# Attention and two MLP layers on one core: values of a batch pooled earlier, PSUM banks 3 and 3, y three chunks behind h

## Chip, cores and metric

One core of a Trainium2 chip runs the whole program. The metric is device time in microseconds (us) of one execution. PE is TensorE (PEld its weight loads), DVE VectorE, ACT ScalarE, POOL GpSimd, SP SyncE.

## What is computed

The reference in short: pooled attention, a dense layer pair, and a layer pair of eight experts with one expert per token.

```python
k_p = k.reshape(8, 8, 72, 8, 64).mean(axis=3)        # keys and values pooled by 8
v_p = v.reshape(8, 8, 72, 8, 64).mean(axis=3)
attn = softmax(q @ k_p^T / 8)                        # 8 batches, 8 heads, 576 queries
x = (attn @ v_p) as [4608, 512]                      # a token's 8 heads side by side
h = x @ w_in                                         # 512 -> 2048
y = maximum(0.01 * h, h) @ w_out                     # 2048 -> 512
expert = argmax(y @ w_gate); gate = softmax(y @ w_gate)[expert]
out = gate * (maximum(y @ w1[expert], 0) @ w2[expert])   # 512 -> 1024 -> 512
```

## The kernel before

The 4608 tokens form 18 blocks of 256, and the 2048 hidden units 16 chunks of 128. One pass of the main loop (L1221) is a step: block b and chunk f. Blocks 0 and 1 take the first 32 steps together; from block 2 on step s is block s // 16, chunk s % 16. All fp32 products are made of pairs of fp32r halves, high and low.

In a step PE makes h of its chunk (`g1`, L495, 12 matmuls of 256 columns) into a PSUM bank. ACT writes 0.01 h into a tile `g`, DVE writes the maximum back into the bank (L509), ACT rounds it to the high half in a `ghl` tile (`g_hi`, L512), and DVE subtracts to get the low half (`g_lo`, L517). PE later makes the chunk's y step (`g2`, L521, 6 matmuls of 512 columns, L529) from `ghl` into banks y0 and y1. The list `pend` holds chunks whose y step is still to come; two are left over after a step, one at the last step of a block and the first of the next. `y_evac` (L536) copies a finished block's y out on ACT in step 0 of the next block.

PSUM has eight banks: two for y, and from step 38 on four for h (h0, h1, and y2 and y3, which the first two blocks' y needed) and two (a0, a1) for all else. `pt` (L124) hands the banks of a kind out in turn, by a counter modulo their number. A new user of a bank waits until the last user's readers are done.

Between h and the y steps of a step, `run_slot` issues what a table has put there (`at`, L1023; `plan`, L1026). Its entries for the attention of token tile t of 128: transposes of q (`att_a`, L361) in chunk 0 or 7, scores (`att_b`), exponential, the quotient `pn` (`att_n`, L401), its transposes (`att_c`, L412 and L418, whose results DVE takes from PSUM to `at_t`), and in chunk 15 the product with the values for the next block (`att_av`, L439). Keys and values of a batch come in seven loads: four of keys, two of values, and the last 64 rows of values. `kv_load` (L190) issues a load on SP into one of two `kv` tiles, `kv_pool` (L290) adds on DVE, three instructions each (L297), and `kv_use` (L308) writes `kT` (by a transpose, L313), `vm` (L325) and `vr`. For the last rows POOL multiplies by a mask (L300), then ACT and DVE write `vr` (`v_rest`, L332). A batch's seven uses stand four of keys first and then three of values, two steps apart:

```python
use += [use[3] + 2, use[3] + 4, use[3] + 6]
```

For batches 2, 3, 6 and 7 the last of these is step 62, 94, 206 and 238, one step ahead of the product that reads it; for batches 4 and 5 it is 135 and 167, eight steps ahead of the product.

The gate's 16 logits of a block are made on DVE (`logit`, L546), about one per step, while the next block is computed; `route_a`, `route_b` and `route_c` then make ranks and scatter the tokens into a list in DRAM. The weights of the experts are split into halves meanwhile: `ps_split` (L824) on ACT and POOL, 128 times. For the first 16 blocks a count (`early_1`) and a list (`early_2`) are made within the last block, at its chunks 7 and 12, and the rows of the first two pairs of tiles are gathered on POOL's DMA queue. After the loop come the last block's routing, 14 pairs of tiles of experts (`p_g1`, `p_h`, `p_g2`) and single tiles (`steps`).

## Time and profile before

| | us |
|---|---|
| three timed runs | 1524.16, 1524.62, 1536.25 |
| median | 1524.62 |
| the profiled execution | 1533.83 |
| its span, first to last instruction | 1532.1 |
| PE busy in it | 1468.8 |
| DVE, ACT, POOL busy | 929.5, 619.1, 337.5 |

All rows shown are of the profiled execution. In the timeline a row is one instruction or several of a kind in a row: start in us, length in us, engine, line, operation, tiles written and read, shape, count; in brackets the idle time of the engine before it and what ended it. Ends of matmuls are modelled and overlap the next start a little.

### The profile page before, as it was taken

What the parts mean: (1) busy time and instruction counts of PE and PEld (TensorE: products, weight loads), DVE (VectorE), ACT (ScalarE), POOL (GpSimd) and SP (SyncE); (2) the same over time, 40 slices, a digit from 0 to 9 for tenths busy, and PEclk for the clock granted to TensorE, in tenths of its full rate; (3) what the DMA queues carried; (4) which work ended last, traced back from release to release, by engine and by line L of the source; (5) the groups of instructions that cost most, each with busy time, mean ns of one, the idle gap of its engine ahead of it and who ended that gap; (6) DMA issues with size and microseconds to landing.
All of it is one profiled execution on the core that took longest, in us unless ns stands there. A gap on an engine that the chain in (4) does not pass through costs nothing. (4 is left out here: it accounts for less than half of the span.)

```text
span 1532.1 us, 25665 instructions
## 1 busy us (share of the span) xinstructions
PE 1468.8 (96%) x9272; PEld 1315.8 (86%) x9272; DVE 929.5 (61%) x2387; ACT 619.1 (40%) x1412; POOL 337.5 (22%) x318
## 2 busy tenths in 40 slices
PE   4698999999999999999999999999999999999998
PEld 3587889999898898899989899988899999988886
DVE  6999588878869888877867867674212112111111
ACT  4666344544444444544444444332222222222222
POOL 4002022222332222222222332111211211201111
PEclk8799999999999999999989999999999999999999
DMA  9543346446445555545636544143611118566160
GB/s 216 148 152 92 111 132 195 163 161 194 162 152 182 169 178 170 174 148 176 193 120 199 172 146 164 49 174 104 275 49 49 56 35 338 202 234 263 42 258 19
DMA packets 121385, 238.05 MB, mean 155 GB/s; under 512 B 56845, under 2 KB 65041, under 8 KB 117544
## 3 DMA queue, kind: packets, MB, share of 16 engines
q1 hardware_dynamic: 90312, 139.81, 29.2%
q10 hardware_dynamic: 23328, 76.56, 13.3%
q0 software_dynamic: 7616, 20.01, 3.9%
q8 instruction: 75, 1.23, 0.3%
q14 instruction: 54, 0.44, 0.1%
HBM read 317.78 MB, written 87.38 MB: 264 GB/s over the span
## 5 line engine op out<-in xcount | busy, mean ns | idle before, releaser
L529 PE MATMUL y<-w,ghl 128*128 128x512 f32 x1728 | 464.4, 406 | 0.9 <-DVE spf L781 0.6
L529 PEld LDWEIGHTS y<-w,ghl 128*128 128x128 f32 x1728 | 309.7, 191 | 58.5 <-DVE ghl L135 3.1
L135 POOL TENSOR_TENSOR ps<-ps 128x512 f32<-128x512 f32 x128 | 181.8, 1421 | 473.6 <-ACT ps L132 391.2
L501 PEld LDWEIGHTS h<-x_t,w 128*128 128x128 f32 x1776 | 236.0, 192 | 32.3 <-DVE w L135 13.6
L501 PE MATMUL h<-x_t,w 128*128 128x256 f32 x1776 | 242.7, 286 | 16.4 <-DVE w L135 12.2
L549 DVE CUSTOM_DVE_ANT_0 junk<-y,wg 128x512 bf16<-128x512 f32 x256 | 201.3, 786 | 2.0
L501 PEld LDWEIGHTS y<-x_t,w 128*128 128x128 f32 x1488 | 193.2, 189 | 9.6
L501 PE MATMUL y<-x_t,w 128*128 128x256 f32 x1488 | 196.2, 282 | 0.0
L951 PE MATMUL y<-w,ghl 128*128 128x512 f32 x672 | 175.1, 399 | 1.0 <-DVE ghl L939 1.0
L951 PEld LDWEIGHTS y<-w,ghl 128*128 128x128 f32 x672 | 119.6, 189 | 22.3 <-DVE ghl L939 1.4
L132 ACT ACTIVATE g<-h 128x256 f32<-128x256 f32 x164 | 62.8, 383 | 151.7 <-PE h L501 140.9
L1007 POOL DMA_INDIRECT out_dram<-kv,sidx x40 | 40.3, 1007 | 372.3 <-ACT kv L1006 188.1
L939 DVE SCALAR_TENSOR_TENSOR ghl<-h,ghl 128x256 fp32r<-128x256 f32 x56 | 23.8, 425 | 136.0 <-ACT ghl L938 136.0
L509 DVE TENSOR_TENSOR h<-g,h 128x256 f32<-128x256 f32 x132 | 56.0, 424 | 77.1 <-ACT g L132 76.4
L135 DVE TENSOR_TENSOR at_t<-a,at_t 128x512 fp32r<-128x512 f32 x62 | 42.7, 688 | 86.9 <-ACT at_t L132 86.4
L132 ACT ACTIVATE ghl<-h 128x256 fp32r<-128x256 f32 x132 | 50.7, 384 | 94.3 <-PE y L529 47.0
L132 ACT ACTIVATE ps<-ps 128x512 fp32r<-128x512 f32 x128 | 80.4, 628 | 15.5 <-DMA ps<-in_moe_w_dram 9.8
L132 ACT ACTIVATE ghl<-y 128x256 fp32r<-128x256 f32 x124 | 47.3, 382 | 94.1 <-DVE y L509 50.6
L132 ACT ACTIVATE g<-y 128x256 f32<-128x256 f32 x124 | 47.4, 382 | 61.4 <-PE y L501 53.8
L135 DVE TENSOR_TENSOR ghl<-h,ghl 128x256 fp32r<-128x256 f32 x132 | 55.5, 420 | 24.8 <-ACT ghl L132 24.5
L616 POOL DMA_INDIRECT lst<-ent,six x36 | 37.7, 1048 | 148.3 <-DVE six L615 110.0
L297 DVE TENSOR_TENSOR kv<-kv 72x512 f32<-72x512 f32 (+8 forms) x126 | 67.9, 539 | 3.2
(272 smaller groups left out, 2140.7 us busy)
## 6 DMA issues: line engine op xcount, KB each, us to landing
w<-wsp SPq DMA_DIRECT2D x108, 2048.0 KB
wsp<-ps ACTq DMA_DIRECT2D x128, 512.0 KB
ps<-in_moe_w_dram SPq DMA_DIRECT2D x128, 256.0 KB
y_d<-y ACTq DMA_DIRECT2D x18, 512.0 KB
raw<-in_moe_w_in_dram SPq DMA_DIRECT2D x16, 512.0 KB
raw<-in_moe_w_out_dram SPq DMA_DIRECT2D x16, 512.0 KB
q<-in_q_dram SPq DMA_DIRECT2D x28, 256.0 KB
kv<-in_k_dram SPq DMA_DIRECT2D x24, 288.0 KB
```

What stands on the lines that cost most here:

```text
L132: nc.scalar.activation(o, i, AF.Copy, scale=scale)
L135: eng.tensor_tensor(out=o, in0=a, in1=b, op=ALU.subtract)
L297: eng.tensor_tensor(out=o, in0=t[:, :, 0:w], in1=t[:, :, w:2 * w], op=ALU.add)
L501: nc.tensor.matmul(p[:, 0:BLK], win(f)[:, kk, l], xv[:, kk, r], start=(n == 0), stop=(n == 3 * KD - 1))
L509: nc.vector.tensor_tensor(out=g, in0=t, in1=h, op=ALU.max)
L529: nc.tensor.matmul(y_ps[b, i], hl[:, l, i * P:i * P + P], wout(f)[:, r], start=(f == 0 and l + r == 0), stop=(last and l == 1),)
L549: nc.vector.tensor_tensor_reduce(out=jk, in0=y_sb[b][:, i], in1=wg_t[0][:, e], scale=1.0, scalar=0.0, op0=ALU.mult, op1=ALU.add, accum_out ...
L616: nc.gpsimd.indirect_dma_start(out=lst, out_offset=bass.IndirectOffsetOnAxis(ap=ix[:, 0:1], axis=0), in_=ent[:, i, :], in_offset=None, bou ...
L939: nc.vector.scalar_tensor_tensor(out=hl[:, 1], in0=b, scalar=0.0, in1=f32(hl[:, 0]), op0=ALU.max, op1=ALU.subtract)
L951: nc.tensor.matmul(o_ps[2 * p + i], hl[:, l, i * P:i * P + P], w[:, r], start=(f == 0 and l + r == 0), stop=(f == 7 and l == 1),)
L1007: nc.gpsimd.indirect_dma_start(out=out, out_offset=bass.IndirectOffsetOnAxis(ap=sidx[:, t:t + 1], axis=0), in_=o, in_offset=None, bounds_c ...
```

## The change

Six edits.

- Values sooner: for batches 3 to 7 the three steps of values stand 7, 5 and 3 steps ahead of the first key step; loads follow the new order. Batch 2 keeps its steps. The masked last rows stand in the same `kv` tile as their source.
- Banks: from step 39 on y2 goes to h and y3 to the rest, three each.
- y three chunks behind h from block 3 on: `pend` keeps three, two at the last step of a block and one at the first of the next. A third `ghl` tile comes with it; the tiles are taken in turn by a counter.
- The `g` tile is one from block 2 on, and the low half of block 1's last chunk is made at once.
- The sixteenth block (b = 15): its logits stand two per step, its routing 6 and 8 steps sooner; `early_1` stands at the step before the last block and `early_2` at its chunk 4.
- The constants `band` and `rep8` stand in a pool that is given back after block 1.

```diff
@@ kv_load
-            t = sb([64, 1, 512], F32, "kv", 2)
+            t = sb([64, 2, 512], F32, "kv", 2)
...
+            kv_raw[nb, 7] = t[:, 1].rearrange("p (h d) -> p h d", h=H)
+        kv_raw[nb, i] = t if i < 6 else t[:, 0:1]
@@ kv_pool
-            f = kv_raw[nb, 7] if nb < 2 else sb([64, H, 64], F32, "kv", 2)
+            f = kv_raw[nb, 7]
@@ g1, g_hi, p_h
+    g_t = [pool.tile([P, BLK], F32, name="g0")]
+    hl_t = [pool.tile([P, 2, BLK], F32R, name=f"ghl{i}") for i in range(2)]
+    hl_n = [0]
+    def hl_next():
+        hl_n[0] += 1
+        return hl_t[hl_n[0] % len(hl_t)]
...
-        t = sb([P, BLK], F32, "g", 2)
+        t = g_t[len(g_n) % len(g_t)]
+        g_n.append(0)
...
-        hl = sb([P, 2, BLK], F32R, "ghl", 2)
+        hl = hl_next()
@@ plan
-            use += [use[3] + 2, use[3] + 4, use[3] + 6]
-            for i in range(7):
-                at(use[i], kv_use, nb, i)
-                if i + 2 < 7:
-                    at(use[i], kv_load, nb, i + 2)
-                at(use[i] - 2 + (i > 3), kv_pool, nb, i)
-            at(max(use[0] - 6, 0), kv_load, nb, 0)
-            at(use[0] - 5, kv_load, nb, 1)
+            rows = [use[3] + 2, use[3] + 4, use[3] + 6] if nb == 2 else [use[0] - 7, use[0] - 5, use[0] - 3]
+            steps = sorted([(c, i) for i, c in enumerate(use)] + [(c, 4 + i) for i, c in enumerate(rows)])
+            for n, (c, i) in enumerate(steps):
+                at(c, kv_use, nb, i)
+                if n + 2 < 7:
+                    at(c, kv_load, nb, steps[n + 2][1])
+                at(c - 2 + (i > 3), kv_pool, nb, i)
+            for n in range(2):
+                at(steps[0][0] - 6 + n, kv_load, nb, steps[n][1])
...
+            elif b == NB - 3:
+                ev, r = None, (s + 9, s + 11)
+                lg_at = [s + j // 2 for j in range(16)]
@@ main loop
-            end = s >= 2 * NF - 1 and (s % NF == NF - 1 or s % NF == 0)
-            while len(pend) > (1 if end else 2):
+            deep = 2 if b < 3 else 3
+            if s >= 2 * NF - 1:
+                deep -= (f == NF - 1) + (deep - 1) * (f == 0)
+            while len(pend) > deep:
                 g2(*pend.pop(0))
...
+            if (b, f) == (3, 0):
+                hl_t.append(second[1].tile([P, 2, BLK], F32R, name="ghl2"))
             if (b, f) == (2, 6):
-                banks["h"] += ["y2", "y3"]
+                banks["h"] += ["y2"]
+                banks["att"] += ["y3"]
             g_hi(b, f)
-            if s < 2 * NF + LAG - 1:
+            if s < 2 * NF + LAG - 1 and (b, f) != (1, NF - 1):
                 late.append((b, f))
...
-            if s == k0 + 7:
+            if s == k0 - 1:
                 early_1()
                 w_regs(NR)
-            if s == k0 + 12:
+            if s == k0 + 4:
                 early_2()
```

In the changed kernel's rows line numbers differ: L507 is its L501, L536 its L529, L516 its L509, L133 its L135.

PE, steps 38 and 39 (block 2, chunks 6 and 7), before; h is written by L501, the y steps are L529, and the number behind a tile's name is that of one use of it:

```order
L501 MATMUL h1_1897<-x_t_67,w01_554 128x256 x12
L412 MATMUL a0_1913<-ident_76,pn_1821 128x128 x4
L418 MATMUL a1_1920<-ident_76,pn_1821 32x128 x2
L529 MATMUL y0_1756<-w11_557,ghl_1842 128x512 x2
L529 MATMUL y1_1757<-w11_557,ghl_1842 128x512 x2
L529 MATMUL y0_1756<-w11_557,ghl_1842 128x512
L529 MATMUL y1_1757<-w11_557,ghl_1842 128x512
L501 MATMUL h0_1940<-x_t_67,w01_554 128x256 x12
```

And now:

```order
L507 MATMUL h1_1825<-x_t_67,w01_551 128x256 x12
L410 MATMUL a0_1840<-ident_76,pn_1752 128x128 x4
L416 MATMUL a1_1847<-ident_76,pn_1752 32x128 x2
L536 MATMUL y0_1691<-w11_554,ghl1_88 128x512 x2
L536 MATMUL y1_1692<-w11_554,ghl1_88 128x512 x2
L536 MATMUL y0_1691<-w11_554,ghl1_88 128x512
L536 MATMUL y1_1692<-w11_554,ghl1_88 128x512
L507 MATMUL h1_1866<-x_t_67,w01_551 128x256 x12
```

In step 39 h goes to h1, the bank of step 38, where it went to h0; the transposes of q go to y3.

PE, the start of block 7, steps 112 to 114, before:

```order
L501 MATMUL h1_4982<-x_t_67,w00_301 128x256 x12
L361 MATMUL a0_4998<-ident_76,q_4666 128x128 x4
L529 MATMUL y0_4475<-w13_1162,ghl_4979 128x512 x2
L529 MATMUL y1_4476<-w13_1162,ghl_4979 128x512 x2
L529 MATMUL y0_4475<-w13_1162,ghl_4979 128x512
L529 MATMUL y1_4476<-w13_1162,ghl_4979 128x512
L501 MATMUL y2_5041<-x_t_67,w00_301 128x256 x12
L501 MATMUL y3_5068<-x_t_67,w00_301 128x256 x12
L380 MATMUL a1_5086<-kT1_71,qT_5003 128x144 x2
L380 MATMUL a0_5091<-kT1_71,qT_5003 128x144 x2
```

And now:

```order
L507 MATMUL y2_4778<-x_t_67,w00_305 128x256 x12
L359 MATMUL a1_4793<-ident_76,q_4456 128x128 x4
L536 MATMUL y0_4303<-w13_1127,ghl0_87 128x512 x2
L536 MATMUL y1_4304<-w13_1127,ghl0_87 128x512 x2
L536 MATMUL y0_4303<-w13_1127,ghl0_87 128x512
L536 MATMUL y1_4304<-w13_1127,ghl0_87 128x512
L536 MATMUL y0_4303<-w13_1127,ghl1_88 128x512 x2
L536 MATMUL y1_4304<-w13_1127,ghl1_88 128x512 x2
L536 MATMUL y0_4303<-w13_1127,ghl1_88 128x512
L536 MATMUL y1_4304<-w13_1127,ghl1_88 128x512
L507 MATMUL h0_4845<-x_t_67,w00_305 128x256 x12
L507 MATMUL h1_4874<-x_t_67,w00_305 128x256 x12
```

Step 112 holds two y steps instead of one, and steps 113 and 114 hold none, where step 114 ended with one.

DVE, end of step 113 to the start of step 115, before; L386 is the maximum of the scores, `junk` a logit:

```order
L135 TENSOR_TENSOR ghl_5065<-y2_5041,ghl_5065 128x256
L509 TENSOR_TENSOR y3_5068<-g_5081,y3_5068 128x256
L386 TENSOR_REDUCE st_5085<-a1_5086 128x4
L135 TENSOR_TENSOR pr_5084<-a1_5086,st_5085 128x288
L386 TENSOR_REDUCE st_5085<-a0_5091 128x4
L135 TENSOR_TENSOR pr_5084<-a0_5091,st_5085 128x288
L549 ISA junk_5097,lg_5033<-y4_5034,wg_1663 128x512
L549 ISA lg_5033 128x1
L135 TENSOR_TENSOR ghl_5107<-y3_5068,ghl_5107 128x256
L509 TENSOR_TENSOR h0_5110<-g_5123,h0_5110 128x256
```

And now:

```order
L133 TENSOR_TENSOR ghl0_87<-h0_4845,ghl0_87 128x256
L516 TENSOR_TENSOR h1_4874<-g0_86,h1_4874 128x256
L384 TENSOR_REDUCE st_4890<-y3_4891 128x4
L133 TENSOR_TENSOR pr_4889<-y3_4891,st_4890 128x288
L384 TENSOR_REDUCE st_4890<-a0_4896 128x4
L133 TENSOR_TENSOR pr_4889<-a0_4896,st_4890 128x288
L133 TENSOR_TENSOR vr0_74<-kv_4698,vr0_74 32x256 x2
L556 ISA junk_4910,lg_4838<-y4_4839,wg_1604 128x512
L556 ISA lg_4838 128x1
L133 TENSOR_TENSOR ghl1_88<-h1_4874,ghl1_88 128x256
L516 TENSOR_TENSOR y2_4914<-g0_86,y2_4914 128x256
```

The two splits that write `vr0`, the last values of batch 4, stand between the scores and the logit; three sums (L297 before, L296 now) have come into step 113 ahead of this piece.

## Rows read from the trace of the kernel before

**Rows 1.** The page: busy time by engine; granted clock in 40 slices, tenths

```profile
PE 1468.8 (96%) x9272; PEld 1315.8 (86%) x9272; DVE 929.5 (61%) x2387; ACT 619.1 (40%) x1412; POOL 337.5 (22%) x318
...
PEclk8799999999999999999989999999999999999999
```

**Rows 2.** What PE waited for, 160 to 1100 us: total, times, longest, in us

```profile
PE a L361 <- DVE at_t L135: 5.6, 4, 2.2
PE a L439 <- DVE vr L135: 4.5, 4, 1.7
...
PE a L418 <- DVE rtmp L606: 1.0, 1, 1.0
PE a L916 <- DMA ps<-y_d,gidx: 0.6, 1, 0.6
PE a L313 <- DVE at_t L135: 0.4, 1, 0.4
```

**Rows 3.** Timeline of PE: start, length, instruction, idle before it and releaser

```profile
474.85 0.65 PE L361 MATMUL a<-ident,q 128*128 128x128 f32 x4 [0.83 <-DVE at_t L135]
...
530.02 0.66 PE L361 MATMUL a<-ident,q 128*128 128x128 f32 x4 [1.67 <-DVE at_t L135]
...
582.66 0.66 PE L361 MATMUL a<-ident,q 128*128 128x128 f32 x4 [0.86 <-DVE at_t L135]
...
637.35 0.66 PE L361 MATMUL a<-ident,q 128*128 128x128 f32 x4 [2.19 <-DVE at_t L135]
```

**Rows 4.** Stretches of 20 us: busy of PE, PEld, DVE, ACT, POOL; clock, DMA

```profile
760.00:780.00 20.00, 18.34 (x95) 16.47 (x94) 12.84 (x33) 8.09 (x20) 3.88 (x3) 0.74 0.26 93
...
880.00:900.00 20.00, 18.92 (x110) 17.40 (x111) 11.88 (x35) 8.40 (x20) 3.93 (x3) 0.83 0.40 142
```

**Rows 5.** Timeline of PE, attention product of blocks 4 and 13, next block's first h

```profile
288.02 0.30 PE L439 MATMUL a<-rm_t,vr 128*128 128x128 f32 x1 [0.69 <-DVE vr L135]
...
293.70 0.52 PE L501 MATMUL h<-x_t,w 128*128 128x256 f32 x3
...
769.75 0.40 PE L439 MATMUL a<-rm_t,vr 128*128 128x128 f32 x1 [1.66 <-DVE vr L135]
...
780.18 1.59 PE L501 MATMUL h<-x_t,w 128*128 128x256 f32 x12
```

**Rows 6.** Timeline of PE and DVE, steps 38 and 39

```profile
207.50 1.70 PE L501 MATMUL h<-x_t,w 128*128 128x256 f32 x12 [0.34 <-DVE ghl L135]
...
208.95 0.69 DVE L549 CUSTOM_DVE_ANT_0 junk<-y,wg 128x512 bf16<-128x512 f32 x1
...
210.30 0.42 DVE L135 TENSOR_TENSOR ghl<-h,ghl 128x256 fp32r<-128x256 f32 x1
```

**Rows 7.** Timeline of DVE, POOL and PE, block 7, steps 112 to 118

```profile
457.08 0.42 DVE L135 TENSOR_TENSOR ghl<-h,ghl 128x256 fp32r<-128x256 f32 x1 [0.67 <-ACT ghl L132]
...
463.70 2.44 DVE L297 TENSOR_TENSOR kv<-kv 72x512 f32<-72x512 f32 x3
...
463.89 1.65 POOL L135 TENSOR_TENSOR ps<-ps 128x512 f32<-128x512 f32 x1 [4.31 <-ACT ps L132]
...
467.49 1.63 PE L529 MATMUL y<-w,ghl 128*128 128x512 f32 x6
...
468.56 0.83 DVE L401 TENSOR_TENSOR pn<-pr,st 128x512 f32<-128x512 f32 x2
...
468.96 1.60 PE L501 MATMUL y<-x_t,w 128*128 128x256 f32 x12
...
470.40 0.60 PE L412 MATMUL a<-ident,pn 128*128 128x128 f32 x4
```

**Rows 8.** Timeline of DVE: three sums of the last values, one batch

```profile
765.61 0.99 DVE L297 TENSOR_TENSOR kv<-kv 64x256 f32<-64x256 f32 x3
```

**Rows 9.** DVE's groups by shape, 200 to 1000 us: busy us, mean ns

```profile
L549 DVE CUSTOM_DVE_ANT_0 junk<-y,wg 128x512 bf16<-128x512 f32 x242 | 191.7, 792 | 1.7
...
L135 DVE TENSOR_TENSOR vr<-kv,vr 32x256 fp32r<-32x256 f32 x12 | 7.4, 620 | 7.1 <-ACT vr L132 7.1
```

More of the change, by code (lines that the diff above doesn't have):

```diff
@@ L99 @@
     mask8 = pool.tile([64, E], F32, name="mask8")
-    band = pool.tile([P, 112], F32, name="band")
-    rep8 = pool.tile([64, E, E], F32, name="rep8")
     ebase = pool.tile([P, E], F32, name="ebase")
@@ L210, in kv_load @@
                 )
-        kv_raw[nb, i] = t
+            kv_raw[nb, 7] = t[:, 1].rearrange("p (h d) -> p h d", h=H)
+        kv_raw[nb, i] = t if i < 6 else t[:, 0:1]
     def kv_load0_k(nb):
@@ L305, in kv_pool @@
             )
-            kv_raw[nb, 7] = f
     def kv_use(nb, i):
@@ L491, in w_conv2 @@
         sub(nc.vector, dl, w, f32(dh))
-    g_raw, g_hl, y_ps = {}, {}, {}
+    g_raw, g_hl, y_ps, g_n = {}, {}, {}, []
+    g_t = [pool.tile([P, BLK], F32, name="g0")]
[4 more added lines that the diff above has]
+        return hl_t[hl_n[0] % len(hl_t)]
     def g1(b, f):
@@ L936, in p_h @@
     def p_h(p, f, b):
-        hl = sb([P, 2, BLK], F32R, "ghl", 2)
+        hl = hl_next()
         nc.scalar.activation(hl[:, 0], b, AF.Relu)
@@ L1128 @@
         e_t = [start.tile([P, 1024], U32, name=f"e{i}") for i in range(2)]
+        g_t.insert(0, start.tile([P, BLK], F32, name="g1"))
         ab_t = start.tile([P, 1024], BF16, name="ab_t")
+        band = cvp.tile([P, 112], F32, name="band")
+        rep8 = cvp.tile([64, E, E], F32, name="rep8")
         raw = [cvp.tile([P, 2, 1024], I32, name=f"raw{i}") for i in range(3)]
@@ L1241 @@
             if (b, f) == (1, NF - 1):
+                g_t.pop(0)
                 stack.close()
```

## The prediction, written before the changed kernel was run

> **What bounds the kernel now.** I read the busy shares of the page first: PE is busy for 96% of the span and DVE for 61% [rows 1], so the time is PE's work plus what PE waits. A busy share says nothing on which waits can go, so the view of what PE waited for comes next, in the stretch from 160 to 1100 us, because what lies before 160 us is ahead of the change [rows 2]. The reader is to see two kinds. In one, the attention product (L439) waits for `vr`, the last values of a batch: 4.5 us in four waits. In the other, transposes (L361, L418, L313) wait until DVE has emptied the PSUM bank that they are to write: 5.6, 1.0 and 0.4 us. The timeline of PE places the 5.6: 0.83 and 0.86 in blocks 7 and 9, 1.67 in block 8, 2.19 in block 10 [rows 3]. The clock is third: two stretches of 20 us have a granted clock of 0.74 and 0.83 [rows 4]. With levels of 1.2 and 2.4 GHz that is 10.4 and 6.8 us at the lower one (20 x 0.26 / 0.5, 20 x 0.17 / 0.5). Each begins at a wait for `vr`, of 1.66 us in the first. Its price is read from equal work: from the waiting matmul to the next block's first takes 10.43 us at 769.75 and 5.68 us at 288.02 [rows 5], 4.75 more, 0.46 per us at the lower level. The second stretch then costs 3.1 us, both 7.85.
>
> The profiled execution took 1533.83 us around a span of 1532.1. Without the two stretches it would be 1525.98, which is 1.4 us (0.1%) above the median of the three timed runs, 1524.62. I read this so: the timed runs at 1524 hold no such stretch, and the gain is to be counted in waits, from 1524.62.
>
> **Values sooner.** For batches 3 to 7 nothing is added; the loads, sums and splits of three value tiles move from the seven steps before the attention product to ahead of the keys. The product of blocks 6, 13 and 15 now comes 20 steps after `vr`, not one. Batch 2 stays, and so does its wait of 0.69 [rows 5]; batches 4 and 5 had no wait. Saved: 4.5 - 0.69 = 3.8 us.
>
> **Three banks for the transposes.** A third bank in turn means that a transpose takes the bank used three allocations ago, whose DVE work is older by one allocation. The four waits of [rows 3], 5.55 us together, go, and so do the 1.0 of L418 (step 134) and the 0.4 of L313 (step 46, after the third bank has come), 6.95 us in all. What is late next at the two places of blocks 7 and 9 is DVE itself, below. Each of these nine waits also costs the overlap of PE's matmul ends: a chunk's twelve matmuls last 1.60 us but the next instruction starts after 1.44 [rows 7], so 0.16 more per wait, 1.4 in all. Saved so far: 3.8 + 6.95 + 1.4 = 12.2 us (12.15).
>
> **h from four banks to three, y one step later.** In steady state PE first asked for DVE's low half of a chunk in that chunk's own y step, with two other chunks' h matmuls and two y steps in between. Now it first asks when the bank comes round, with two h and three y steps in between: one y step more patience, 1.47 us from its first matmul at 467.49 to the next chunk [rows 7]. So I count no new wait. The one `g` tile costs nothing: ACT's rounding of a chunk already waits for DVE's maximum, and only then reads the next bank.
>
> One place is different. The banks change while the turn counter runs on. Step 38 uses h1 in both kernels; step 39 used h0 before and uses h1 again now, because 40 modulo 3 is 1. So it waits until DVE has written the low half of step 38. In the trace that instruction runs at 210.30 for 0.42, behind the two logits that start at 208.95; step 39 had begun at 207.50 after a wait of 0.34 [rows 6]. The new start is 210.72, 3.2 us later. ACT and DVE do the same work in this stretch either way, so nothing hides it. Bounds: 3.0, since little in that row of work could close up, and 4.2, if one logit is stretched by 1 us as the sums at 463.70 are [rows 7]. I take 3.2, the row.
>
> The wait of 3.5 us that results is longer than the 1.66 that led to the lower clock, but 2.19 in [rows 3] did not: in the page's slices of 38 us the clock reads 9 tenths or more from the third slice on, but for the one at 766 us [rows 1]. The Trainium skill (TensorE: Matmul & The Clock Gate, HAM oscillation — how this bites in real kernels) says that the throttled clock is the default, that activity releases it and that idle gaps bring it back; by it this gap would bring a stretch at half rate, and the trace agrees for 1.66 and disagrees for 2.19. From rows alone the price lies between 0 and 4.75; I take half of the shorter stretch's 3.1, 1.6 us.
>
> **At the ends of blocks.** With three pending, step 0 of a block now holds two y steps where it held one, and steps 1 and 2 none. The y evacuation on ACT, and with it DVE's logits, come one y step later, 1.47 us. PE's own order contains the same work by step 3, so this costs only where DVE is busy without a gap from there to the softmax quotient `pn` (L401) that step 6 transposes. In blocks 7 and 9 it is: from 457.08 on DVE has no idle row, and `pn` is ready 1.0 us before L412 at 470.40 [rows 7]. Batches 4 and 5 now put values just there: three sums of 0.99 together [rows 8], and two `vr` splits of 0.62 each [rows 9]; their two `vm` splits fall into the idle 0.67 at 457.08. 1.47 + 0.99 + 1.24 - 1.0 = 2.7 us late, in each of two blocks. ACT also stands in its queue for POOL's product before it can write `vr`, and the high half of that step's chunk stands behind it; its bank is asked for only three steps on. DVE's durations move with what runs beside them: three key sums take 2.44 at 463.70, while POOL subtracts, against 0.99 for three narrower ones [rows 7, 8]. So the bounds are 0, if the two meetings that block 7 has now fall away, with 1 us each and some of DVE's waits for ACT, and 3.7, if one more comes. Between them I take 1.5 each, 3.0 together, nearer to the waits of 0.83 and 0.86 that the same backlog made here before.
>
> The rule that speaks against the new places is in the Trainium skill (SBUF — State Buffer, Who interferes with whom): a VectorE instruction with two SBUF inputs and a GpSimd one that reads SBUF exclude each other for a whole instruction. The trace agrees: the key sums at 463.70 take 2.44 us beside POOL's subtraction at 463.89 [rows 7]. By the rule every moved sum that meets one of POOL's subtractions is held for that instruction's whole length, 1.65 us there, so each wait could come out at 2.7 + 1.65 = 4.3 and the sum at 1526.
>
> From blocks 8 and 10 all three value steps leave, the 0.99 and 1.24 among them, so DVE's lag there falls by more than the 1.47 that the block's start adds. Blocks 4, 11 and 13 receive values in steps 6 to 11, where DVE had slack: I count 0, at most 0.5 each.
>
> **The sixteenth block.** Thirteen of its 16 logits move up by one to seven steps, 0.79 us each on DVE [rows 9], and its routing, count, row list and four gathers by six to eight. PE has no wait for them before: the one wait for gathered rows, 0.6 us [rows 2], is that of the third pair, whose list is made after the loop. So nothing is gained; the fetch and gathers on POOL stand ahead of the last routing's scatters, and SP's two register loads wait at a time when it has no other transfer to issue. Cost 0, at most 1 if DVE's list arithmetic delays the first chunks of the last block.
>
> **The sum.** -12.2 + 3.2 + 1.6 + 3.0 = -4.4 us: from the profiled execution without its two stretches, 1525.98, to 1521.6, and from the median, 1524.62, to 1520.2. I forecast 1520.
>
> **Rivals.**
> 1. DVE keeps up. The sums in blocks 7 and 9 meet POOL less, and the wait at step 39 leaves the clock alone: -12.2 + 3.2 = -9.0, 1516. For it: the idle 0.67 and waits of 2.19 without a drop. Against: no gap in DVE's rows of block 7.
> 2. Slower: new waits of PE bring the lower clock. If step 39 and the waits in blocks 7 and 9 (3.7 each) each lead to a stretch like that at 769.75, the change is -12.2 + 3.2 + 7.4 + 3 x 4.75 = +12.7, 1537. With the waits at their largest the balance is -1.6, so the first drop already decides. For it: 1.66 was enough once; against: 2.19 was not, and the waits in one block come in parts.
> 3. The timed runs hold stretches at the lower clock as the profile does, and they go with the `vr` waits: -9.0 - 7.85 = -16.9, 1508. Against it is the sum above, which meets 1524.62 without them.
> 4. The values come no sooner in effect, because the loads stand on SP behind others and the tiles are short: the 3.8 us and their overlap stay, 1524.5. Against it: three steps lie between load and sum, as before.
>
> **How the numbers follow.** My forecast has a chance of 0.47, rivals 1 to 4 have 0.30, 0.11, 0.08 and 0.04. A measurement of this kernel can tell about 1% (15 us) from no change. Over 1% faster is rival 3, 0.08; over 1% slower is the worst of rival 2, 0.03; the rest is 0.89. The range runs from 1511, between rivals 1 and 3, to 1530, which takes in the forecast with both waits at 3.7 and a drop of 4.75 (-12.2 + 3.2 + 7.4 + 4.75 = +3.2, 1528).
>
> **What would show it.** Right: no wait of L439's counterpart for `vr` after batch 2; no wait of transposes for DVE's `at_t` in blocks 8 and 10; one wait of 3 to 4 us before the h matmuls of step 39, released by DVE's `ghl`; waits for `pn` or for an h bank in steps 5 to 7 of blocks 7 and 9. Wrong: step 39 without a wait, or waits for banks in many blocks, which would mean that three h banks are too few.

## The result and the profile after

| | before | after |
|---|---|---|
| median of nine timed runs each, us | 1530.03 (1524.16 to 1540.05) | 1515.55 (1513.21 to 1518.09) |
| ratio, 95% interval | | 0.9901 (0.9884 to 0.9917) |
| the profiled execution, its span | 1533.83, 1532.1 | 1515.57, 1513.9 |
| span up to step 32, from there to step 272, behind it | 182.5, 810.3, 539.3 | 182.2, 797.1, 534.6 |

The time lies in the range and within 1%, if only just. Beside the prediction's sum it does not fit: that sum is made of waits and their price in clock, and the waits hardly changed in total. The page of after, to set against [rows 1]:

```profile
PE 1450.0 (96%) x9272; PEld 1295.5 (86%) x9272; DVE 932.7 (62%) x2387; ACT 609.1 (40%) x1412; POOL 337.3 (22%) x318
...
PEclk8799999999999999999999999999999999999999
```

The same 9272 matmuls keep PE busy for 18.8 us less (1468.8 before), which is the whole change of the span (18.2). What PE waited for in after, 160 to 1100 us (total, times, longest, in us), answers to [rows 2]:

```profile
PE h L507 <- DVE ghl L133: 8.5, 8, 3.7
PE y L507 <- DVE ghl L133: 2.2, 2, 1.4
PE y L958 <- DVE ghl L946: 1.1, 1, 1.1
PE y L311 <- PE h L507: 1.0, 2, 0.5
PE a L437 <- DVE vr L133: 0.9, 1, 0.9
PE a L923 <- DMA ps<-y_d,gidx: 0.5, 1, 0.5
PE a L410 <- DVE pn L399: 0.5, 2, 0.3
```

The kinds turned over as the change has it: `vr` is waited for once (batch 2), `at_t` of L361 (now L359) not at all. But h (L501, now L507) waits 10.7 us for `ghl`, where before had

```profile
PE h L501 <- DVE ghl L135: 1.2, 2, 0.9
```

Added up from step 32 to 272, PE idled 12.8 us before and 13.1 after. Where the new waits are, in PE's timeline of after (start, length, instruction, idle before it):

```profile
209.94 1.43 PE L507 MATMUL h<-x_t,w 128*128 128x256 f32 x5 [3.68 <-DVE ghl L133]
...
339.02 1.22 PE L507 MATMUL h<-x_t,w 128*128 128x256 f32 x8 [0.64 <-DVE ghl L133]
...
464.20 1.63 PE L507 MATMUL h<-x_t,w 128*128 128x256 f32 x12 [0.62 <-DVE ghl L133]
...
468.21 1.65 PE L507 MATMUL h<-x_t,w 128*128 128x256 f32 x12 [0.83 <-DVE ghl L133]
470.37 0.25 PE L311 MATMUL y<-ident,kv 72*128 72x72 f32 x1 [0.51 <-PE h L507]
...
570.02 1.64 PE L507 MATMUL y<-x_t,w 128*128 128x256 f32 x12 [1.44 <-DVE ghl L133]
574.03 1.65 PE L507 MATMUL h<-x_t,w 128*128 128x256 f32 x12 [0.82 <-DVE ghl L133]
```

The first is step 39, the second step 78; then steps 116 and 117 (chunks 4 and 5 of block 7), 148 and 149 (chunks 4 and 5 of block 9). The pace of the matmuls shows best where two chunks of h follow one another without y or a wait, as steps 241 and 242 do in both kernels. Before (PE's timeline):

```profile
893.20 3.02 PE L501 MATMUL y<-x_t,w 128*128 128x256 f32 x24
896.06 1.14 PE L380 MATMUL a<-kT,qT 128*128 128x144 f32 x8
```

After:

```profile
881.23 1.53 PE L507 MATMUL y<-x_t,w 128*128 128x256 f32 x12
882.59 1.53 PE L507 MATMUL h<-x_t,w 128*128 128x256 f32 x12
883.96 0.65 PE L378 MATMUL y<-kT,qT 128*128 128x144 f32 x4
```

From the first start to that of the next line's work, 24 matmuls take 2.86 us before and 2.73 after: 119 and 114 ns each, at a granted clock of 1.00 in both. So it is in every block: start to start, the h matmuls take 119 to 120 ns before in all chunks, 114 after in chunks 0 to 7 of a block and 117 in chunks 8 to 15 (medians over the chunks). Blocks 6 and 15, which have no wait in either kernel, last 51.45 us before and 50.77 after, from their first matmul to the next block's; "a block without waits" below is one of these.

### The profile page after: what moved, and what is told of

Read it like the earlier page. It is cut to its first block, busy times and chain, and to the rows that moved or that the text cites. A ratio compares the mean times of both kernels' runs of the same rounds, so it can differ in the third digit from the quotient of the medians.

```text
span 1513.9 us, 25943 instructions
## 1 busy us (share of the span) xinstructions
PE 1450.0 (96%) x9272; PEld 1295.5 (86%) x9272; DVE 932.7 (62%) x2387; ACT 609.1 (40%) x1412; POOL 337.3 (22%) x318
## 5 line engine op out<-in xcount | busy, mean ns | idle before, releaser
L536 PE MATMUL y<-w,ghl 128*128 128x512 f32 x1728 | 456.6, 402 | 0.7 <-DVE spf L788 0.6
L536 PEld LDWEIGHTS y<-w,ghl 128*128 128x128 f32 x1728 | 307.9, 189 | 57.6 <-DVE ghl L133 1.6
L507 PEld LDWEIGHTS h<-x_t,w 128*128 128x128 f32 x2268 | 294.1, 191 | 43.9 <-DVE w L133 13.8
L507 PE MATMUL h<-x_t,w 128*128 128x256 f32 x2268 | 304.2, 284 | 24.0 <-DVE w L133 12.4
L133 POOL TENSOR_TENSOR ps<-ps 128x512 f32<-128x512 f32 x128 | 180.5, 1410 | 481.1 <-ACT ps L130 429.4
L507 PEld LDWEIGHTS y<-x_t,w 128*128 128x128 f32 x996 | 126.4, 188 | 9.9 <-DVE ghl L133 3.7
L507 PE MATMUL y<-x_t,w 128*128 128x256 f32 x996 | 130.1, 280 | 2.2 <-DVE ghl L133 2.2
L130 ACT ACTIVATE g<-h 128x256 f32<-128x256 f32 x205 | 78.2, 381 | 130.9 <-PE h L507 121.8
L130 ACT ACTIVATE ghl<-h 128x256 fp32r<-128x256 f32 x173 | 66.2, 383 | 131.3 <-DVE h L516 83.5
L516 DVE TENSOR_TENSOR h<-g,h 128x256 f32<-128x256 f32 x173 | 72.9, 421 | 55.8 <-ACT g L130 54.7
L133 DVE TENSOR_TENSOR ghl<-h,ghl 128x256 fp32r<-128x256 f32 x173 | 72.5, 419 | 28.6 <-ACT ghl L130 26.7
L133 DVE TENSOR_TENSOR at_t<-a,at_t 128x512 fp32r<-128x512 f32 x49 | 33.7, 688 | 87.3 <-ACT at_t L130 87.2
L296 DVE TENSOR_TENSOR kv<-kv 72x512 f32<-72x512 f32 (+8 forms) x126 | 73.7, 585 | 3.2
L1013 ACT ACTIVATE kv<-y,gate 128x512 f32<-128x512 f32 x40 | 26.0, 686 | 94.5 <-PE y L958 67.1
L937 PEld LDWEIGHTS h<-at_t,w 128*128 128x128 f32 x456 | 58.1, 188 | 3.0
```

Source lines behind the costliest of these rows:

```text
L130: nc.scalar.activation(o, i, AF.Copy, scale=scale)
L133: eng.tensor_tensor(out=o, in0=a, in1=b, op=ALU.subtract)
L296: eng.tensor_tensor(out=o, in0=t[:, :, 0:w], in1=t[:, :, w:2 * w], op=ALU.add)
L507: nc.tensor.matmul(p[:, 0:BLK], win(f)[:, kk, l], xv[:, kk, r], start=(n == 0), stop=(n == 3 * KD - 1))
L516: nc.vector.tensor_tensor(out=g, in0=t, in1=h, op=ALU.max)
L536: nc.tensor.matmul(y_ps[b, i], hl[:, l, i * P:i * P + P], wout(f)[:, r], start=(f == 0 and l + r == 0), stop=(last and l == 1),)
```

## The experiments

**Where the pace comes from.** The change also moves tiles in SBUF: `band` and `rep8` leave the main pool, `g` and `ghl` become fixed tiles ahead of the weights. `x_t` and `at_t` stay at 128 (addresses modulo 256 here and below); the weights of chunks 0 to 7 go from 128 to 192, those of chunks 8 to 15 from 32 to 96, `ghl` from 128 to 224 (the third one, new from block 3 on, stands at 64). The first run takes these places into the kernel before, and with them what belongs to the fixed tiles: one `g` tile from block 2 on and the low half of block 1's last chunk at once. It has no third `ghl`; order, banks and loads stay otherwise. Only a part of its edit is shown.

```diff
-    band = pool.tile([P, 112], F32, name="band")
-    rep8 = pool.tile([64, E, E], F32, name="rep8")
...
+    g_t = [pool.tile([P, BLK], F32, name="g0")]
+    hl_t = [pool.tile([P, 2, BLK], F32R, name=f"ghl{i}") for i in range(2)]
...
+        band = cvp.tile([P, 112], F32, name="band")
+        rep8 = cvp.tile([64, E, E], F32, name="rep8")
```

> The kernel before with the change's SBUF placement alone: band and rep8 in the pool of the first stage, g and ghl as fixed tiles ahead of the weights, so that x_t stays where it was and every weight tile stands at the same address as in the changed kernel; order, banks and loads as before. Theory 'placement' (the pace of the 256-column h matmuls hangs on where their weights lie against x_t): start to start of those matmuls 114 ns for chunks 0 to 7 and 117 ns for chunks 8 to 15 in place of 120 ns, a block without waits 50.8 us in place of 51.45 us, the waits of before all still there, and the time 12 to 15 us under the kernel before (ratio about 0.991). Rival 'order and banks' (three h banks, y three slots behind, or the new issue order give the pace): 120 ns, 51.45 us, ratio 1.000 within 0.002.

Measured: ratio 0.9945 (0.9921 to 0.9969), 1520.32 us. Chunks 0 to 7 run at 114 ns, chunks 8 to 15 at 117, blocks without any wait, 51.4 to 51.6 us before, last 50.7 to 51.0, and the old waits stand in the main (`vr` 5.2 us in four; 13.5 us of idle PE from step 32 to 272 in all). Steps 241 and 242 take 2.75 us:

```profile
883.48 2.91 PE L506 MATMUL y<-x_t,w 128*128 128x256 f32 x24
886.23 1.14 PE L378 MATMUL a<-kT,qT 128*128 128x144 f32 x8
```

The pace is the placement's; neither banks nor order is needed for it. The gain in time was smaller than expected, 8.4 us (4.7 to 12.1). A part of what is missing can be clock: the mean granted clock of its seven runs is 0.9806, of the twelve of before beside them 0.9831. That is 7.6 us more at the lower level, by the prediction's 0.46 an estimated 3.5 us.

The reverse: the changed kernel with its schedule, and the weights and all three `ghl` back at the places modulo 256 of before.

```diff
-    iota8 = pool.tile([P, E], F32, name="iota8")
-    rev8 = pool.tile([P, E], F32, name="rev8")
-    prow = pool.tile([P, 1], F32, name="prow")
...
     hl_t = [pool.tile([P, 2, BLK], F32R, name=f"ghl{i}") for i in range(2)]
+    iota8 = pool.tile([P, E], F32, name="iota8")
+    rev8 = pool.tile([P, E], F32, name="rev8")
+    prow = pool.tile([P, 1], F32, name="prow")
...
-    mb = pool.tile([P, 1], F32, name="mb")
-    rank0 = pool.tile([P, E], F32, name="rank0")
...
+                mb = pool.tile([P, 1], F32, name="mb")
+                rank0 = pool.tile([P, E], F32, name="rank0")
+                t = second[1].tile([P, 2 * BLK + 48], F32R, name="ghl2")
```

> The changed kernel with all weights and ghl back at the places modulo 256 that they had before the change (ghl 128; weights of chunks 0 to 7 at 128, of chunks 8 to 15 at 32), by moving five small tiles; its schedule is the changed one. Theory 'placement': 120 ns again in all chunks, and what is left of the gain is the scheduling's: the placement alone gave 0.9945, so 0.9901 / 0.9945 = 0.9956, 1523.5 us, 4 to 10 us under the kernel before. Rival (the schedule gives the rest of the pace as well): 114 and 117 ns, 0.990.

Measured: ratio 0.9996 (0.998 to 1.0012), 1530.89 us. As before 119 to 120 ns in all chunks, a block without waits 51.5 us:

```profile
889.17 1.59 PE L507 MATMUL y<-x_t,w 128*128 128x256 f32 x12
890.60 1.60 PE L507 MATMUL h<-x_t,w 128*128 128x256 f32 x12
892.03 0.65 PE L375 MATMUL y<-kT,qT 128*128 128x144 f32 x4
```

Moving five small tiles, and the third `ghl` by some padding, takes the whole gain away. The schedule alone is worth 0.6 us here (3.1 us to -1.8); by the first run it would be 0.9901 / 0.9945 = 0.9956, some 7 us, 2 to 11 with the two intervals. The two overlap between 2 and 3 us: nearer the runs don't come to the schedule's share, and the placement's is the larger.

**What in the placement.** Three kernels run matmuls alone. The first: runs of h with the weights moved on by 32 bytes at a time, then runs of y.

```python
for d in range(64):
    h_run(0, 8 * d)
```

> Matmuls alone, nothing of the computation: runs of 12 h matmuls (256 columns, the twelve operand pairs of one chunk) whose weights lie 0, 32, 64 ... 2016 bytes further on against a fixed moving tile, twice; sixteen of them again with the moving tile 224 bytes further on; and runs of 6 y matmuls (512 columns) with the moving weights 0, 32 ... 2016 bytes further on. Theory 'placement': the mean start to start of a run changes with the distance alone, between about 113 and 120 ns in the h runs, with the same values in both passes, about 120 ns where the distance is that of before (512 bytes, modulo 2048) and about 113.5 ns at that of the changed kernel (832 bytes); the y runs spread likewise around 232 ns. Rival 'order and banks': all distances within 1 ns of each other.

Measured: the pace repeats every 256 bytes, and with the moving tile shifted as well the two distances tried (32 and 160) give the same pace within 0.5 ns. At distances 0, 32 ... 224 it is 119.1, 118.3, 118.0, 117.5, 119.8, 119.8, 117.8 and 118.6 ns; y goes from 228.7 to 235.2. So the distance matters, but the changed kernel's (64) gives 118.0, not 113.5: something was missing. The second kernel turns h and y runs as the real one does.

```python
for a in range(8):
    for b in range(8):
        for rep in range(3):
            h_run(X0 + 8 * a, W0 + 8 * b)
            y_run(G0 + 8 * a, V0 + 8 * b)
```

> Matmuls alone, nothing of the computation: a chunk's twelve h matmuls and six y matmuls in turn, as in the kernel, at the addresses of the kernel's tiles; the moving h tile at 8 places 32 bytes apart and the h weights at 8 places 32 bytes apart, all 64 pairs, three chunks each (the y matmuls with ghl and their weights likewise), and eight pairs again with the h weights 55 KB lower. In the run of h matmuls alone the pace repeated every 256 bytes but did not reach the 113.5 ns of the changed kernel. Theory 'both places, modulo 256, and the turn of h and y runs': the pair of before (128, 128) gives 120 ns in the steady part of a chunk, (128, 32) 119.8, the changed kernel's (128, 192) 113.5 and (128, 96) 117, and the pairs with weights 55 KB lower the same as their twins. Rival 'something else of the kernel (other engines' traffic, high address bits)': all pairs between 117.5 and 120 as in the run of h matmuls alone, no 113.5.

Measured, with a pair written as (h tile, h weights): (128, 128) has 120 ns in the steady part, as before. (128, 192) has 118 in all three chunks beside `ghl` at 128. In the last eight pairs, with `ghl` at 224 and the weights 55 KB lower, it has 118 in two chunks and 113.5 in the third, at the same places. Both theories miss. The third kernel holds the h tile at 128 and tries all triples (h weights, `ghl`, y weights).

```python
for g in range(8):
    for b in range(8):
        for v in range(8):
            for rep in range(2):
                chunk(W0 + 8 * b, G0 + 8 * g, V0 + 8 * v)
```

> Matmuls alone, nothing of the computation: chunks of twelve h and six y matmuls in turn with the moving h tile at 128 (modulo 256), and h weights, ghl and y weights each at 8 places 32 bytes apart, all 512 triples, two chunks each. In the grid before this one the same pair of h tile and h weights (128, 192) gave 118 ns beside ghl at 128 and 113 ns beside ghl at 224. Theory (the pace of h hangs on all four places, because the weight loads of y and h run ahead into one another): (192, 224, 192), the changed kernel's chunks 0 to 7, gives 113 to 114 ns in the steady part, (96, 224, 96), its chunks 8 to 15, 117; (128, 128, 128), before's, 120; and among the 512 there are triples whose whole chunk is shorter than any of these, by up to 30 ns of 2750. Rival (the 113 ns of the first grid came of the lower addresses of those weights): no triple at 113 to 114, (192, 224, 192) at 118.

Measured, as the second of each triple's two chunks: (192, 224, 192) gives 113 to 114 ns in its steady part and 2767 ns a chunk, (96, 224, 96) 2785, (128, 128, 128) 120 ns and 2820, (32, 128, 32) 2840. The 512 triples, the map below, go from 2734 to 2855. Timeline of two chunks, first (128, 128, 128), then (192, 224, 192), with no other engine at work:

```profile
1705.02 1.59 PE L47 MATMUL b<-reg 128*128 128x256 f32 x12
1706.45 1.55 PE L52 MATMUL b<-reg 128*128 128x512 f32 x6
1707.84 0.40 PE L47 MATMUL b<-reg 128*128 128x256 f32 x2
...
2885.08 1.54 PE L47 MATMUL b<-reg 128*128 128x256 f32 x12
2886.45 1.55 PE L52 MATMUL b<-reg 128*128 128x512 f32 x6
2887.84 0.40 PE L47 MATMUL b<-reg 128*128 128x256 f32 x2
```

The h run takes 1.43 us at the one and 1.37 at the other, first start to the y run's. But a single chunk is not the measure of its places. In a quarter of the triples the two chunks differ by more than 15 ns, once by 71, and with the h weights at 192 the steady pace has two levels, 113 and 118 ns: in 24 of those 64 triples one chunk runs at the one and one at the other. Here (192, 192, 192), its first chunk and its second:

```profile
2522.53 1.58 PE L47 MATMUL b<-reg 128*128 128x256 f32 x12
2523.94 1.55 PE L52 MATMUL b<-reg 128*128 128x512 f32 x6
2525.33 1.54 PE L47 MATMUL b<-reg 128*128 128x256 f32 x12
2526.71 1.54 PE L52 MATMUL b<-reg 128*128 128x512 f32 x6
```

What stands out of this scatter is the place of the h weights: the mean chunk (64 triples, both chunks) takes 2784 ns with them at 192, 2799 at 96, 2823 at 128 and 2828 at 32. By the place of `ghl` the means go from 2807 to 2811 only, by that of the y weights from 2807 to 2812. With these means a block of 16 chunks would gain 0.54 us by the changed places; the block without waits gained 0.68. So the place of the h weights against the h tile makes the larger part of the pace; that `ghl` and the y weights count too is not shown by this map, and neither is why places count at all. Does the map serve to choose places? The next run puts weights and all three `ghl` at 192 in the changed kernel.

```diff
     hl_t = [pool.tile([P, 2, BLK], F32R, name=f"ghl{i}") for i in range(2)]
+    prow = pool.tile([P, 1], F32, name="prow")
+    st_t = pool.tile([P, 3, H], F32, name="st")
...
+                t = second[1].tile([P, 2 * BLK + 32], F32R, name="ghl2")
```

> The changed kernel with one small tile moved behind ghl and st in front of the weights, so that all weights and the three ghl stand at 192 modulo 256 (ghl was at 224, 224 and 64, the weights of chunks 8 to 15 at 96); nothing else. Theory 'placement': by the second grid a chunk takes 2752 ns at (192, 192, 192) against 2767 and 2785 at the changed kernel's two triples and 2793 in the expert stage, together 10.7 us; the same map gave 17.6 us for the step from before's places to the changed kernel's, of which the run with the placement alone showed about 9, so half of it here too: 5 us, with 10.7 as the other end; ratio to the kernel before 0.983 to 0.987, h matmuls 113 to 115 ns in all chunks. Rival (the map does not carry over to other places): 0.990, as the changed kernel.

Measured: ratio 0.9878 (0.9855 to 0.99), 1512.01 us; between the two, and its interval meets that of after. The expectation went by the triple's second chunk, with 114.75 ns for its h matmuls; its first has 117.7, and 117.7 is the median of the chunks in the kernel. A block without waits stays at 50.75 us, and only the stretch behind step 272 is shorter, 532.5 us for 534.6. Chunks 0 to 7 show the two levels here as well. At the lower, 113 ns, run 104 of the 127 that can be read in after, 104 of 128 in e1_place and 30 of 127 here. The h tile, the h weights and the y weights of these chunks stand where they do in after; `ghl` and a few small tiles have moved. So something besides the h operands decides between the levels, `ghl`'s place for all that is known, and the map could not foretell it. It tells these bad places from the good ones; it does not rank the good ones.

**The wait at step 39.** One line moves the turn of the h banks on where the third comes in.

```diff
                 banks["att"] += ["y3"]
+                turn["h"] += 1
```

> The changed kernel with the turn of the h banks moved on by one where the third bank comes in, so that step 39 takes y2 and not the bank that step 38 has just filled. Theory: the wait of 3.68 us in step 39 goes, and with it the 3.4 us at half clock right behind it (some 1.7 us lost), no wait comes in its place, so 5.4 us under the changed kernel: ratio to the kernel before about 0.9866. Rival (DVE and ACT are behind at step 39 whatever bank is taken, and the next steps wait instead): waits over 3 us by ghl in steps 40 to 42, ratio 0.990 as the changed kernel.

Measured: ratio 0.9871 (0.9849 to 0.9893), 1510.74 us. The wait is gone and none comes in its place: block 2 lasts 54.68 us, where it lasts 59.96 in after. The clock: two windows of after (busy time of PE, PEld, DVE, ACT and POOL, then the granted clock, DMA share, GB/s),

```profile
200.00:220.00 20.00, 16.32 (x106) 14.87 (x105) 13.66 (x45) 7.82 (x20) 4.47 (x3) 0.91 0.45 150
285.00:305.00 20.00, 19.11 (x125) 17.50 (x124) 12.36 (x38) 9.32 (x22) 5.58 (x4) 0.91 0.37 111
```

and the same windows here:

```profile
200.00:220.00 20.00, 20.00 (x139) 18.36 (x138) 17.38 (x57) 9.49 (x23) 5.82 (x5) 1.00 0.60 201
285.00:305.00 20.00, 20.00 (x138) 18.37 (x138) 14.67 (x47) 9.26 (x21) 4.27 (x3) 1.00 0.66 207
```

0.91 is 3.6 us at the lower level, at the prediction's 0.46 a price of 1.7: with the wait, 5.3 us, which is what block 2 lost. In all six profiles with this wait (after, e4_v45, e6_two_behind, e8_late_list, e10_place192 and e12_old) the clock is at the lower level for 3.4 us from about the wait's end on. The second window's drop has no such tie: in after it follows the wait of 0.89 for `vr`, and here the same wait, 1.16, brings none.

With the places of e10_place192 too:

> The kernel of e10_place192 with the turn of the h banks moved on by one where the third bank comes in, as in e3_turn. Theory: the two gains add up, ratio 0.980 to 0.984 (e3_turn had 0.9871). Rival (faster matmuls only make PE wait longer for DVE): 0.986 to 0.988, with longer waits in blocks 7, 9, 12 and 13.

Measured: ratio 0.9854 (0.983 to 0.9878), 1509.02 us: under before and after, 1.5% below before, between what the two expected, and not to be told from e3_turn's 0.9871. The waits are not longer (9.9 us from step 32 to 272, 14.1 without the turn).

**The values of batches 4 and 5.**

```diff
-            rows = [use[3] + 2, use[3] + 4, use[3] + 6] if nb == 2 else [use[0] - 7, use[0] - 5, use[0] - 3]
+            rows = [use[3] + 2, use[3] + 4, use[3] + 6] if nb in (2, 4, 5) else [use[0] - 7, use[0] - 5, use[0] - 3]
```

> The changed kernel with the values of batches 4 and 5 back at their old steps behind the keys (batches 3, 6 and 7 stay sooner). Theory (the pooling of the values ahead of the softmax of the same block makes DVE late in blocks 7 and 9): the waits of steps 116, 117 and 148 to 149 (1.45 and 2.26 us) and the half microseconds behind them go, no wait for vr comes at the ends of blocks 8 and 10, because batches 4 and 5 had none before either: 4 us or so under the changed kernel, ratio about 0.9875. Rival (the three banks or y three behind make those waits): both blocks as in the changed kernel, ratio 0.990.

Measured: ratio 0.9888 (0.987 to 0.9907), 1514.02 us. The waits in blocks 7 and 9 go (51.69 and 51.74 us for 54.03 and 54.88) and none for `vr` comes; but blocks 8 and 10 now wait for `ghl` and `pn` and last 54.09 and 54.65 us for 50.94 and 52.97:

```profile
524.21 0.63 PE L410 MATMUL a<-ident,pn 128*128 128x128 f32 x4 [0.59 <-DVE pn L399]
527.34 1.65 PE L507 MATMUL h<-x_t,w 128*128 128x256 f32 x12 [0.90 <-DVE ghl L133]
...
632.08 1.66 PE L507 MATMUL h<-x_t,w 128*128 128x256 f32 x12 [0.87 <-DVE ghl L133]
```

The four blocks together are 0.65 us shorter. In either place PE waits for DVE; moving DVE's work moved the wait.

**The third slot of y.**

```diff
-            deep = 2 if b < 3 else 3
+            deep = 2
```

> The changed kernel with y two slots behind h throughout, as before the change; three banks each and the rest as changed. Theory (of the prediction: the third slot gives a bank of h one y step more of patience, about 1.5 us): new waits of h matmuls for ghl in blocks whose DVE is late, 3 to 8 us in all, ratio to the kernel before 0.992 to 0.995. Rival (the third slot only makes y and with it the logits later at each block's start): no new waits, the waits in blocks 7 and 9 shorter, ratio 0.988.

Measured: ratio 0.9917 (0.9893 to 0.9942), 1517.76 us; between the two, and its interval meets that of after. In all PE waits as long (13.4 us; more in block 11, none in block 16), but from block 3 on at y instead of h:

```profile
PE y L536 <- DVE ghl L133: 6.1, 7, 1.4
PE h L507 <- DVE ghl L133: 4.6, 2, 3.7
PE y L536 <- ACT ghl L130: 1.8, 2, 1.5
```

**The third bank of the transposes.**

```diff
-                banks["h"] += ["y2"]
-                banks["att"] += ["y3"]
+                banks["h"] += ["y2", "y3"]
```

> The changed kernel with the two banks that come in at step 38 both given to h, as before: four for h, two for the transposes. Theory (the prediction's: the third bank of the transposes takes their waits): the waits of transposes for at_t come back in blocks 7 to 10, up to 5.6 us, and those at step 39 and its half clock (5.4 us) go, so that the two cancel: ratio about 0.990. Rival (the values' new places alone have taken the waits for at_t, by emptying blocks 8 and 10 of them): no waits for at_t in blocks 8 and 10, no wait in step 39, ratio 0.986.

Measured: ratio 0.9986 (0.997 to 1.0003), 1528.24 us: far over what either expected. Step 39 waits 0.4 us, but PE idles 23.1 us from step 32 to 272:

```profile
PE a L311 <- DVE at_t L133: 8.5, 4, 3.0
PE a L359 <- DVE at_t L133: 5.8, 4, 2.5
PE a L311 <- issue: 3.8, 2, 1.9
PE a L610 <- DVE pr L133: 1.7, 2, 1.3
```

The keys' transposes (L311), which waited 0.4 us in before, now meet DVE's backlog too; two banks don't bear that. So the third bank and the rest of the schedule belong together. Which part of it, the values' new places or y's third slot, brings the backlog there is not shown.

**The sixteenth block.** Its routing, the list and the gathers back at the old steps (the branch of `NB - 3` left out, `k0 + 7` and `k0 + 12` again).

> The changed kernel with the routing of the sixteenth block, the first row list and the first gathers at their old steps. Theory (nothing waited for them; the 4.7 us that the stretch after step 272 became shorter by are the faster h matmuls of the expert stage): ratio 0.990 as the changed kernel, the stretch after step 272 still about 534.6 us. Rival (the earlier list lets the expert stage start sooner): that stretch 537 to 539 us, ratio 0.992 to 0.993.

Measured: ratio 0.9902 (0.9879 to 0.9925), 1514.99 us; the stretch behind step 272 takes 535.9 us, 1.3 more, by one wait of 1.16 for gathered rows. No difference in time: the 4.7 us there are the faster matmuls, for the stretch takes 534.6 us in e1_place, with the old list and the new places, and 539.9 in e12_old, with the new list and the old places.

## Why the prediction was right, and where not

It was right in the time, and that was luck: the larger part of the gain is in no term of its sum. The measured 1515.55 even meets rival 1's 1516, whose conditions failed: DVE did not keep up, and step 39 did lower the clock. Its steps in turn:

**The base.** What fell is 1524.62 as the time to count from, and with it the reading that the timed runs hold no such stretch as the profiled one. Two of the first three runs were among the lowest of all; the median over nine is 1530, and over the 17 of the last comparison 1531.69. Of these 17, those with a mean granted clock of 0.985 or more took 1528.0 to 1528.9, those of 0.98 or less 1531.9 to 1538.4. So most of before's executions seem to hold stretches at the lower level, as rival 3 has it, if not all as many as the profiled one (16.8 us in steps 32 to 272 by windows of 10 us; after 6.2).

**Values sooner.** Right: 4.5 us of `vr` become 0.9, and the first stretch of [rows 4], which began at that wait of 1.66, goes with it.

**Three banks for the transposes.** Right: of the waits counted there none is left. In the new schedule the third bank is worth more than the 6.95, 12.7 us between the medians of after and e7_four_banks, although the latter has no long wait at step 39; but that is for other waits, most of them the keys' transposes.

**Step 39.** Right to half a microsecond: a wait of 3.68 by `ghl` (3.2 more and 0.34 that was there), and 1.7 us of clock where 1.6 were put down between bounds of 0 and 4.75. That the clock met is luck: half of the shorter stretch had no row behind it.

**h from four banks to three.** "I count no new wait" is not what came: besides step 39, h now waits for its bank in blocks 4, 7, 9, 11 and 13 (and 0.24 in 16). The prediction's own sign for too few banks, waits for banks in many blocks, was partly met. With y two behind (e6_two_behind) PE waits in all as long at y, so at these places DVE is late for either. Whether a fourth h bank beside three for the transposes would take the waits, no run shows.

**Blocks 7 and 9.** Waits in the blocks named, but 1.96 and 2.77 us for 1.5 each, and in chunks 4 and 5 for an h bank, where `pn` at chunk 6 was worked out to be late and steps 5 to 7 were named.

**Blocks 4, 11 and 13: "0, at most 0.5 each".** Wrong: 0.64, 0.80 and 1.08 (in e8_late_list, which changes nothing in these blocks, 0.22, 0.80 and 0.67). The step that failed is the price of DVE's work beside POOL. It was weighed for the value sums, but the new work ahead of a logit moves the logit onto POOL as well. In block 4 that work is the two `vr` splits, as DVE's and POOL's timeline of after at step 78 shows:

```profile
336.01 0.87 DVE L133 TENSOR_TENSOR vr<-kv,vr 32x256 fp32r<-32x256 f32 x2
336.90 1.71 DVE L556 CUSTOM_DVE_ANT_0 junk<-y,wg 128x512 bf16<-128x512 f32 x1
...
336.77 1.30 POOL L133 TENSOR_TENSOR ps<-ps 128x512 f32<-128x512 f32 x1 [2.54 <-issue]
```

In block 7, at step 116, it is the value sums, and POOL's product for the last rows stands there too:

```profile
460.42 0.68 DVE L556 CUSTOM_DVE_ANT_0 junk<-y,wg 128x512 bf16<-128x512 f32 x1
...
461.14 2.66 DVE L556 CUSTOM_DVE_ANT_0 junk<-y,wg 128x512 bf16<-128x512 f32 x1
463.73 0.41 DVE L133 TENSOR_TENSOR ghl<-h,ghl 128x256 fp32r<-128x256 f32 x1
...
460.63 1.37 POOL L299 TENSOR_TENSOR kv<-kv,mask 64x512 f32<-64x512 f32 x1 [7.83 <-DMA ps<-in_moe_w_dram]
461.96 1.29 POOL L133 TENSOR_TENSOR ps<-ps 128x512 f32<-128x512 f32 x1
```

A logit takes 0.68 us where most of it runs alone, 1.71 beside POOL's subtraction and 2.66 beside product and subtraction; `ghl`, for which PE waits at 464.20, stands right behind it. At steps 190 and 222 it is as at step 78. No run takes the splits of blocks 4, 11 and 13 away again; for these three the cause is read from the rows. The rule that the prediction cited (the Trainium skill, SBUF — State Buffer, Who interferes with whom) names these pairs, and the trace agrees; it was applied to the moved instructions and not to those that they push.

**The sixteenth block.** Right: nothing.

**The sum.** It has -4.4 us for the schedule. Measured with the placement taken out: 0.6 us less (e12_old, with 3.1 less as its far end) or 7 less (after against e1_place). So -4.4 lies between two runs that don't agree, and is not confirmed; its make-up differs. In the profiles, from before to e12_old, waits give 1.3 us and the clock 4.6 (10.0 us less at the lower level, at 0.46).

**What no term holds.** The edits of `band`, `rep8`, `g` and `ghl` were read for their buffers alone ("the one `g` tile costs nothing"), and not for where they put every tile allocated behind them. That is the larger part: by the timed runs 8.4 us (4.7 to 12.1) in the old schedule, and some 14.5 in the new one, where the ratios to before are 0.9996 and 0.9901; by the profiled spans 15.8 and 14.3. That the first of these two pairs differs so much is not settled, but for the clock's part named above. The prediction still came within 5 us of the median, because its base was 5.4 us too low: the drop itself was put at 4.4 and measured some 15.

## What to carry to other kernels

An edit that adds or removes a small tile moves all tiles behind it; compare the addresses of the matmul operands and the start-to-start pace of one clean run of matmuls before any wait is given credit for a difference. Where DVE is the late engine, moving its work moves the wait: look at what stands behind the moved instruction and beside POOL. When a rotation changes its length while its counter runs on, work out which bank the next step takes.

## What the runs showed that was not expected

The pace of 256-column fp32r matmuls at a granted clock of 1.00 depends on where the operands lie in SBUF. In runs of h alone it repeats every 256 bytes of distance between weights and moving tile, from 117.5 to 119.8 ns from start to start. Between runs of y it goes from 113 to 120 ns, and the mean chunk of twelve h and six y matmuls from 2784 to 2828 ns by the place of the h weights. The places do not fix it wholly: with the weights at 192 a chunk runs at 113 or at 118 ns, with the same operands both occur, and in the kernel 104 of 127 or 30 of 127 chunks had the lower, by what else had moved. So a map of single chunks misleads by up to 5 ns a matmul; read each place several times.
